# A list scheduler that plans each engine's order: another model of the DMA queue in its play-through

## The chip, the cores and the metric

The kernel runs on one core of a Trainium2 chip. The metric is the device time of one execution in microseconds (us); a kernel's time is the median of several executions. TensorE is called PE in the profile, VectorE DVE, ScalarE ACT, GpSimd POOL and SyncE SP.

## The reference

For batch 8, 8 heads, 576 positions and head size 64, a causal attention with a window of 64 positions is followed by a gated channel mix over rows of 512 values (all heads side by side):

```python
scores = np.where(mask, scale * (q @ k.T), -1e9)     # mask: 0 <= row - column < 64
attn = exp(scores - max) / (sum + 1e-9)
x = (attn @ v)                                       # heads joined: (8, 576, 512)
x_prev = x shifted by one position within each batch
xk = mu_k * x + (1 - mu_k) * x_prev
xr = mu_r * x + (1 - mu_r) * x_prev
k = np.maximum(xk @ w_k, 0)                          # (8, 576, 1024)
out = sigmoid(xr @ w_r) * ((k * k) @ w_v)
```

q, k and v are float32; the three weights come as 64-bit floats, of which the kernel reads the bits.

## The kernel before

**Tiles.** The 4608 rows (8 x 576) are cut into nine units u of 512 rows, and the 512 columns into four chunks c of 128 (two heads). A pair (u, c) is a *group*, numbered g = 4u + c, 36 in all. For a group, `scores` multiplies q with k in 32 small matmuls (into two banks), `soften` takes row minima (`least`, on DVE; the trace calls them CUSTOM_DVE_ANT_0, the order ISA) and exponentials (`exp`, ACT), `shares` turns the row sums into reciprocals (`rs`), `scale` applies them (POOL or DVE), `flip` transposes the weights on PE, `keep` copies the result out of its bank (`pt`), and `values` multiplies with v; `keep_x` copies that into `xT`.

**Units.** Per unit, `mix` blends xT with itself shifted by one row: `d` on ACT, then DVE, then a split into a high and a low part `xs` (each product is made of three matmuls: high by high, high by low, low by high). `r_units` multiplies with w_r, `k_units` with w_k, then relu, square, split (`ks`), and `v_units` multiplies `ks` with w_v; DVE gates the result and SP stores it. These products, 2160 matmuls of 128x512 in all, are the bulk of PE's work. In the trace they are `bank<-xs,ws` (w_r and w_k) and `bank<-ks,ws` (w_v).

**Weights.** There are 20 chunks of 128 x 512 values, 512 KB each as 64-bit words: four of w_r, eight of w_k, eight of w_v. `decode` turns each into a high and a low float (`ws`): `sign` on ACT, then on DVE `clamp` and three bitwise operations (`shift`, `top`, `low`), through a bank, then `first_part` on ACT and `second_part` on POOL or DVE. Only one chunk at a time may be between `shift` and `low` (room "bits": 1).

**What sets the order.** The code does not issue instructions as it goes. Every step is a `Piece` (L82) with an engine (or a choice of two), a key (its due place), a cost in ns, the pieces it needs, and the buffers it takes and frees. `play()` (L96) then plays through the whole program against these costs: on each engine, whenever it is free, the piece with the lowest key begins whose needs are done and landed and whose buffers are free. Behind a piece's end stands its `lag`, the time until others can use what it made. The order in which pieces begin is the order in which the instructions are written (L706), and it is fixed: each engine takes its instructions strictly in this order on the chip, whatever comes late. All instructions are issued through one helper, so the profile gives L69 for nearly all of them.

**Loads.** All loads and stores are issued by SP. `transfer` (L266) makes the piece of a load. The loads at the start have no key and go first, in the order of the calls at L652 to L665: the k and q of groups 0 to 3, the v of groups 0 to 3, the four chunks of w_r between them, then eight chunks of w_k and eight of w_v. For these, `transfer` adds the bytes up at 300 bytes a ns and gives each the sum as its landing time. The loads of groups 4 and up carry a key (one or two places ahead of their group's `burst`), go as soon as their buffer is free, and are taken to land 2000 ns after they are issued, whatever is in the queue ahead of them. An issue costs SP 60 ns in the plan. Groups 2 and 3 have buffers of their own for k and q (`qks`, from the pool of `xs`), so group 4 uses the buffer of group 0 and group 5 that of group 1.

**Bursts.** `burst` is PE's piece of attention: scores of a group, transposes of another, values of a third. The first four have keys -30 to -27, group 4 has -8 (`begin`, L668).

Of the kernel before, what the change touches and what calls it, by code (L numbers as in the profile page):

```python
# [14 lines left out]
ALU = mybir.AluOpType  # L15
PSUM = bass.MemoryType.PSUM

P = 128
# [6 lines left out]
UB = 8  # L25
NU = B * NB // UB
TU = UB * W
# [16 lines left out]
LINK = 80  # L44

HI_MIN = struct.unpack("<f", struct.pack("<I", 0x38000000))[0]
HI_MAX = struct.unpack("<f", struct.pack("<I", 0x47EFFE00))[0]
# [3 lines left out]
def attn_rwkv_kernel(ctx, tc, qT, kT, v2, mu_k, mu_r, w_k, w_v, w_r, out):  # L51
# [9 lines left out]
    class Engine:  # L61


        def __init__(self, engine):
            self.engine = engine
# [5 lines left out]
    pe, dve, sca, pool, dma = (Engine(e) for e in (nc.tensor, nc.vector, nc.scalar, nc.gpsimd, nc.sync))  # L71
    room = {"tmp": TB, "bank": 8, "m": 4, "bits": 1, "s": 2, "t": 2, "x": 1, "pr": 4, "sums": 4, "pt": 4, "xT": XB,
            "xs": SB, "r": R_BUFS, "qk": 2, "v": 3}
    pieces = []
# [7 lines left out]
    class Piece:  # L82


        def __init__(self, engine, key, cost, fn, needs=(), takes=(), uses=(), lag=LINK, spare=0, port=False):
            self.costs = engine if isinstance(engine, dict) else {engine: cost}
            self.home = next(iter(self.costs))
            self.engine, self.key, self.fn = None, key, fn
            self.needs = [p for p in needs if p is not None]
            self.takes, self.uses, self.lag, self.spare, self.port = list(takes), list(uses), lag, spare, port  # L90
            for hold in (*self.takes, *self.uses):
                hold.users.append(self)
            self.done = None
            pieces.append(self)

    def play():  # L96

        left, free, now, begun, port = {}, {}, 0, [], 0
        for n, p in enumerate(pieces):
            for e in p.costs:  # L100
                left.setdefault(e, []).append((p.key, n, p))
                free[e] = 0
        for e in left:
            left[e].sort(key=lambda x: (x[2].home != e, *x[:2]))
        users = {id(h): len(h.users) for p in pieces for h in p.takes}
        ends = []
        times = [0]
        while any(left.values()):
            assert times, [(e, [(p.key, p.fn.__name__) for _, _, p in ps[:4]]) for e, ps in left.items()]
            now = heapq.heappop(times)  # L110
            while ends and ends[0][0] <= now:
                _, _, p = heapq.heappop(ends)
                for hold in (*p.takes, *p.uses):
                    users[id(hold)] -= 1
                    if not users[id(hold)]:
                        room[hold.tag] += 1
            for e, ps in left.items():
                if free[e] > now:
                    continue
                for _, n, p in ps:  # L120
                    if not all(q.done is not None and q.done + (q.lag if q.engine != e else 30) <= now for q in p.needs):
                        continue
                    tags = [h.tag for h in p.takes]
                    if any(room[tag] < tags.count(tag) + (p.spare if tag == "m" else 0) for tag in set(tags)):
                        continue
                    locks = e == "POOL" or (e == "DVE" and p.port)
                    if locks and port > now:
                        continue
                    if p.home != e and max(free[p.home], now) + p.costs[p.home] < now + p.costs[e]:
                        continue  # L130
                    for o in p.costs:
                        left[o].remove((p.key, n, p))
                    for tag in tags:
                        room[tag] -= 1
                    p.engine = e
                    free[e] = p.done = now + p.costs[e]
                    if locks:
                        port = p.done
                    begun.append(p)
                    for at in (p.done, p.done + 30, p.done + p.lag):  # L140
                        heapq.heappush(times, at)
                    heapq.heappush(ends, (p.done + p.lag, n, p))
                    break
        return begun
# [5 lines left out]
        return 150 + 0.52 * n  # L150

    def act_ns(n):
        return 95 + 0.86 * n

    def pool_ns(n):
        return 195 + 2.1 * n
# [1 line left out]
    engines = {"DVE": dve, "POOL": pool}  # L158
# [63 lines left out]
    def decode(n, loaded):  # L222
        ws, _, i, c = chunks[n]
        key = DECODE[n]
        word, bits = Hold("tmp"), [Hold("bank"), Hold("bits")]

        def sign(e):
            words[n] = tmp.tile([P, WC], F32, name="wt", tag="tmp", bufs=TB)
            sca.activation(words[n], raw[n][:, :, 1].bitcast(F32), AF.Abs)

        def clamp(e):
            dve.tensor_scalar(words[n], words[n], HI_MIN, HI_MAX, op0=ALU.max, op1=ALU.min)

        def shift(e):
            words[n, 0] = bank(WC).bitcast(U32)
            dve.tensor_scalar(words[n, 0], words[n].bitcast(U32), 3, 0x3FFFFFF8,
                              op0=ALU.logical_shift_left, op1=ALU.bitwise_and)

        def top(e):
            dve.scalar_tensor_tensor(words[n, 0], raw[n][:, :, 1], 0xC0000000, words[n, 0],  # L240
                                     op0=ALU.bitwise_and, op1=ALU.bitwise_or)

        def low(e):
            dve.scalar_tensor_tensor(words[n].bitcast(U32), raw[n][:, :, 0], 29, words[n, 0],
                                     op0=ALU.logical_shift_right, op1=ALU.bitwise_or)

        def first_part(e):
            ws[i, c] = const.tile([P, 2, WC], F32R, name="ws", tag="w", bufs=len(chunks))
            sca.copy(ws[i, c][:, 0], words[n])

        def second_part(e):
            engines[e].tensor_sub(ws[i, c][:, 1], words[n], ws[i, c][:, 0].bitcast(F32))

        p = Piece("ACT", key, 600, sign, [loaded], takes=[word])
        p = Piece("DVE", key, 430, clamp, [p], port=True)
        p = Piece("DVE", key, 700, shift, [p], takes=bits)
        p = Piece("DVE", key, 700, top, [p])
        p = Piece("DVE", key, 700, low, [p], uses=bits)
        p0 = Piece("ACT", key, 560, first_part, [p])
        decoded[id(ws), i, c] = p0, Piece({"POOL": 1270, "DVE": 700}, key, 0, second_part, [p0], uses=[word], port=True)  # L260


    loaded, arrived, held = {}, {}, {}
    bus = [0]

    def transfer(fn, size, takes=(), needs=(), key=None):  # L266

        p = Piece("SP", len(pieces) - 9999 if key is None else key, 60, fn, needs, takes, lag=2000)
        if key is None:
            bus[0] = max(bus[0], 1300) + size / 300  # L270
            p.lag = bus[0] + 900
        return p


    groups = [(u, c) for u in range(NU) for c in range(NC)]
# [29 lines left out]
    def load_qk(g, key=None):  # L305
        u, c = groups[g]
        held[g] = [Hold("xs" if g in (2, 3) else "qk")]

        def load(e):
            if g in (2, 3):  # L310
                both = act.tile([P, 2, TU], F32, name="qks", tag="xs", bufs=SB)
                loaded[g] = [both[:, 0], both[:, 1]]
            else:
                loaded[g] = [ld.tile([P, TU], F32, name="q"), ld.tile([P, TU + 2 * W], F32, name="k")]
            q, k = loaded[g]
            for b, k0, k1, o in key_loads[u]:
                dma.dma_start(k[:, o * W:(o + k1 - k0) * W], kT[b * NP + c, :, k0 * W:k1 * W])
            o = 0
            for b, i0, i1 in stretches(u):
                n = i1 + 1 - i0  # L320
                dma.dma_start(q[:, o * W:(o + n) * W], qT[b * NP + c, :, i0 * W:(i1 + 1) * W])
                o += n

        arrived[g] = transfer(load, 4 * P * 2 * TU, held[g], key=key)

    def load_v(g, key=None):
        u, c = groups[g]
        held["v", g] = [Hold("xs" if g == 3 else "v")]

        def load(e):  # L330
            if g == 3:
                loaded["v", g] = act.tile([P, UB, P], F32, name="vs", tag="xs", bufs=SB)
            else:
                loaded["v", g] = ld.tile([P, UB, P], F32, name="v", bufs=3)
            for b, a, c0, c1, o in value_loads[u]:
                dma.dma_start(loaded["v", g][:, o:o + c1 - c0], v2[b * NP + c, :, a, c0:c1])

        arrived["v", g] = transfer(load, 4 * P * P * UB, held["v", g], key=key)

    banks, weights, sums, flipped = {}, {}, {}, {}  # L340
    xTs, got = {}, {}
# [316 lines left out]
    load_v(1)  # L658
    load_w(1)
    load_qk(3)  # L660
    arrived["mu"] = Piece("DVE", -25, 300, rest, [transfer(vectors, 4096)])
    load_v(2)
    load_w(1)
    load_v(3)
# [74 lines left out]
```

## Time and profile before

| | us |
|---|---|
| median of 3 executions | 698.28 (697.80 to 699.03) |
| the profiled execution | 697.61 |
| its span, first to last instruction | 695.8 |
| TensorE busy | 633.5 |
| DVE busy | 413.8 |
| ACT busy | 415.6 |
| POOL busy | 112.8 |

The page gives one execution, divided into 40 equal slices; a digit is the busy share of an engine in tenths. A timeline row has the start, the duration, the engine, the line, the operation with its output and inputs, a count of merged instructions and, in brackets, the idle time before and what ended it. Busy time of DVE counts overlapping instructions once, so the step from one start to the next can be shorter than an instruction's duration. A row of the waits reads: who waited for whom, total, times, longest.

### The profile page before, as it was taken

To read this page: it belongs to the slowest core of one execution; us is meant where nothing else is said; L and a number is where in the kernel's file an instruction comes from. 1 tells how busy PE (TensorE), PEld (TensorE's weight loads), DVE (VectorE), ACT (ScalarE), POOL (GpSimd) and SP (SyncE) were. 2 spreads that over 40 slices of the span, in tenths; PEclk is the share of its full clock that TensorE was granted. 3 is DMA by queue.
4 is the path that set the end of the run, shared out by engine and by line. 5 is a ranking of instruction groups with operands and counts; after the bars stand their busy time and mean duration, and the time that the engine had idled before them with its cause. 6 is when DMAs were issued, how large, how long until landed. Compare 5 with 4: busy or idle time off the path is not lost.

```text
span 695.8 us, 12937 instructions
## 1 busy us (share of the span) xinstructions
PE 633.5 (91%) x4752; PEld 510.0 (73%) x4752; DVE 413.8 (59%) x1194; ACT 415.6 (60%) x1130; POOL 112.8 (16%) x183
## 2 busy tenths in 40 slices
PE   1058687899999999999999999999999999999997
PEld 0036565787788888888888888888888888888886
DVE  1047999968758556754675467646764676353311
ACT  2049866947887368646754775477647764671540
POOL 2027784520001000200020002000200020000000
PEclk9998999999999999999999999999999999999999
DMA  8952200244122222222122123222322230001001
GB/s 316 401 183 84 56 1 0 72 151 134 59 60 90 90 60 59 90 90 61 59 90 90 60 59 105 76 65 65 114 80 71 67 112 29 1 16 45 1 0 61
DMA packets 47583, 57.87 MB, mean 83 GB/s; under 512 B 7584, under 2 KB 39328, under 8 KB 47520
## 3 DMA queue, kind: packets, MB, share of 16 engines
q1 hardware_dynamic: 47520, 57.04, 25.4%
q8 instruction: 38, 0.62, 0.4%
q14 instruction: 25, 0.20, 0.1%
HBM read 47.58 MB, written 9.44 MB: 82 GB/s over the span
## 4 chain that ended last, share of the span: by engine, by line
PE 79%; DVE 8%; DMA 5%; ACT 3%; issue 2%; POOL 1%; SPq 0%; DVEq 0%
PE bank L69 79%; DVE bank L69 3%; DVE wt L69 2%; DMA w<-w_v 2%; ACT pr L69 1%; DVE pr L69 1%; DMA q<-qT 1%; DMA w<-w_k 1%; DMA qks<-qT 1%; DMA v<-v 1%; DVE d L69 1%; POOL pr L69 1%; DVE r L69 1%; SPq L69 0%; ACT d L69 0%
## 5 line engine op out<-in xcount | busy, mean ns | idle before, releaser
L69 PE MATMUL bank<-xs,ws 128*128 128x512 f32 x1296 | 316.5, 400 | 9.3 <-ACT xs L69 3.5
L69 PEld LDWEIGHTS bank<-xs,ws 128*128 128x128 f32 x1296 | 244.1, 190 | 68.6 <-ACT xs L69 4.7
L69 PE MATMUL bank<-ks,ws 128*128 128x512 f32 x864 | 209.1, 396 | 1.7 <-ACT xT L69 1.7
L69 PEld LDWEIGHTS bank<-ks,ws 128*128 128x128 f32 x864 | 161.6, 188 | 38.8 <-ACT xT L69 2.1
L69 ACT ACTIVATE pr<-pr,nmax 128x128 f32<-128x128 f32 x288 | 111.9, 393 | 42.5 <-DVE nmax L69 42.4
L69 DVE TENSOR_TENSOR ks<-kf,ks 128x512 fp32r<-128x512 f32 x66 | 45.6, 692 | 82.3 <-ACT ks L69 81.0
L69 PE MATMUL bank<-k,q 64*64 64x128 f32 x1088 | 41.5, 289 | 40.0 <-DMA q<-qT 39.4
L69 ACT ACTIVATE kf<-bank 128x512 f32<-128x512 f32 x72 | 43.0, 599 | 48.6 <-PE bank L69 45.9
L69 PEld LDWEIGHTS bank<-k,q 64*64 64x64 f32 x1088 | 32.4, 140 | 52.3 <-DMA q<-qT 35.8
L69 ACT COPY xT<-bank 128x512 f32<-128x512 f32 x35 | 20.6, 588 | 77.0 <-PE bank L69 76.9
L69 DVE SCALAR_TENSOR_TENSOR r<-bank,r 128x512 f32<-128x512 f32 x36 | 24.9, 692 | 60.7 <-PE bank L69 60.6
L69 DVE CUSTOM_DVE_ANT_0 pr<-bank,maskNone 128x128 f32<-128x128 f32 x224 | 53.7, 286 | 10.5 <-PE bank L69 10.5
L69 ACT ACTIVATE th<-bank 128x512 f32<-128x512 f32 x36 | 21.5, 598 | 63.7 <-PE bank L69 59.6
L69 POOL TENSOR_SCALAR pr<-pr,rs 128x128 f32<-128x128 f32 x76 | 31.8, 437 | 162.8 <-ACT d L69 90.9
L69 ACT ACTIVATION_READ_ACCUMULATOR pr<-pr,nmax 128x1 f32 x288 | 54.9, 191 | 0.0
L69 POOL TENSOR_TENSOR kf<-kf 128x512 f32<-128x512 f32 x12 | 12.5, 1041 | 253.9 <-ACT kf L69 253.9
L69 PE MATMUL bank<-ident,pr 128*128 128x128 f32 x288 | 44.1, 290 | 6.1 <-POOL pr L69 3.3
L69 ACT CAST xs<-d 128x512 fp32r<-128x512 f32 x72 | 43.8, 618 | 3.7 <-DVE d L69 1.6
L69 ACT CAST ks<-kf 128x512 fp32r<-128x512 f32 x72 | 44.2, 617 | 1.7
L69 DVE CUSTOM_DVE_ANT_0 pr<-bank,mask 128x128 f32<-128x128 f32 x64 | 17.9, 286 | 44.3 <-PE bank L69 44.3
L69 PEld LDWEIGHTS bank<-pt,v 128*64 128x64 f32 x1120 | 37.2, 142 | 8.2 <-issue 5.5
L69 PE MATMUL bank<-pt,v 128*64 128x64 f32 x1120 | 42.3, 230 | 1.0 <-ACT kf L69 0.5
(54 smaller groups left out, 585.3 us busy)
## 6 DMA issues: line engine op xcount, KB each, us to landing
v<-v SPq DMA_DIRECT2D x31, 192.0 KB, 2.8
w<-w_k SPq DMA_DIRECT2D x8, 512.0 KB, 8.0
w<-w_v SPq DMA_DIRECT2D x8, 512.0 KB, 10.4
v<-v SPq DMA_DIRECT2D x32, 128.0 KB, 2.4
v<-v SPq DMA_DIRECT2D x15, 256.0 KB, 3.9
v<-v SPq DMA_DIRECT2D x36, 64.0 KB, 2.4
w<-w_r SPq DMA_DIRECT2D x4, 512.0 KB, 5.6
outT<-r SPq DMA_DIRECT2D x8, 256.0 KB, 2.0
```

Source lines behind the costliest of these rows:

```text
L69: return lambda *args, **kw: tc.keep_in_program_order(op(*args, **kw))
```

## The change

In the play-through a piece may now have a `size`. When a piece with a size begins, `play()` keeps one running time for the bus: the later of the bus's time and the end of issue, plus the bytes at 380 a ns; the load lands 2000 ns after that. This goes for every transfer made by `load_w`, `load_qk`, `load_v` and `vectors`, with a key or without; a store keeps its fixed lag of 2500 ns. An issue costs 470 ns for each DMA that the piece issues (`dmas`) instead of 60 ns. Two edits go with it: the plan's cost of an ACT operation is 95 + 0.94 n ns instead of 95 + 0.86 n, and `clamp` takes the minimum first and then the maximum, with its engine given as a choice of one.

```diff
-        def __init__(self, engine, key, cost, fn, needs=(), takes=(), uses=(), lag=LINK, spare=0, port=False):
+        def __init__(self, engine, key, cost, fn, needs=(), takes=(), uses=(), lag=LINK, spare=0, port=False, size=0):
...
-        left, free, now, begun, port = {}, {}, 0, [], 0
+        left, free, now, begun, port, bus = {}, {}, 0, [], 0, 0
...
+                    if p.size:
+                        bus = max(bus, p.done) + p.size / 380
+                        p.lag = bus - p.done + 2000
...
     def act_ns(n):
-        return 95 + 0.86 * n
+        return 95 + 0.94 * n
...
-            dve.tensor_scalar(words[n], words[n], HI_MIN, HI_MAX, op0=ALU.max, op1=ALU.min)
+            engines[e].tensor_scalar(words[n], words[n], HI_MAX, HI_MIN, op0=ALU.min, op1=ALU.max)
...
-        p = Piece("DVE", key, 430, clamp, [p], port=True)
+        p = Piece({"DVE": 430}, key, 0, clamp, [p], port=True)
...
-    bus = [0]
-
-    def transfer(fn, size, takes=(), needs=(), key=None):
-
-        p = Piece("SP", len(pieces) - 9999 if key is None else key, 60, fn, needs, takes, lag=2000)
-        if key is None:
-            bus[0] = max(bus[0], 1300) + size / 300
-            p.lag = bus[0] + 900
-        return p
+
+    def transfer(fn, size, takes=(), needs=(), key=None, dmas=1):
+
+        return Piece("SP", len(pieces) - 9999 if key is None else key, 470 * dmas, fn, needs, takes, size=size)
...
-        arrived[g] = transfer(load, 4 * P * 2 * TU, held[g], key=key)
+        arrived[g] = transfer(load, 4 * P * 2 * TU, held[g], key=key, dmas=2 * len(key_loads[u]))
...
-        arrived["v", g] = transfer(load, 4 * P * P * UB, held["v", g], key=key)
+        arrived["v", g] = transfer(load, 4 * P * P * UB, held["v", g], key=key, dmas=len(value_loads[u]))
...
-    arrived["mu"] = Piece("DVE", -25, 300, rest, [transfer(vectors, 4096)])
+    arrived["mu"] = Piece("DVE", -25, 300, rest, [transfer(vectors, 4096, dmas=2)])
```

More of the change, by code (lines that the diff above doesn't have):

```diff
@@ L89, in __init__ @@
             self.needs = [p for p in needs if p is not None]
-            self.takes, self.uses, self.lag, self.spare, self.port = list(takes), list(uses), lag, spare, port
+            self.takes, self.uses, self.lag, self.spare, self.port, self.size = list(takes), list(uses), lag, spare, port, size
             for hold in (*self.takes, *self.uses):
```

## The prediction

> **What bounds the kernel now.** I read the page first, then the timelines of the load queue and of TensorE, then the chain and the waits, then stretches of time.
>
> The page: engine totals and the span in 40 slices of 17.4 us.
>
> ```profile
> span 695.8 us, 12937 instructions
> PE 633.5 (91%) x4752; PEld 510.0 (73%) x4752; DVE 413.8 (59%) x1194; ACT 415.6 (60%) x1130; POOL 112.8 (16%) x183
> PE   1058687899999999999999999999999999999997
> DVE  1047999968758556754675467646764676353311
> DMA  8952200244122222222122123222322230001001
> ```
>
> PE is full from the ninth slice to the end; of its 62.3 us of idle time (695.8 - 633.5) nearly all lies before. In the second slice every engine but DMA stands at or near 0; after it DVE is full for four slices while PE is not. So there are two stages to explain: a stop, and a start-up carried by DVE.
>
> TensorE's timeline (start, duration, engine, operation, count, idle before and its releaser), then the end of the chain of waits:
>
> ```profile
> 4.22 1.98 PE L69 MATMUL bank<-k,q 64*64 64x128 f32 x32 [4.22 <-DMA q<-qT]
> 41.38 2.44 PE L69 MATMUL bank<-k,q 64*64 64x128 f32 x32 [35.18 <-DMA q<-qT]
> ...
> 127.25 7.24 PE L69 MATMUL bank<-ks,ws 128*128 128x512 f32 x30 [1.66 <-ACT xT L69]
> 134.43 1.10 PE L69 MATMUL bank<-k,q 64*64 64x128 f32 x32
> ```
> ```profile
> 34.14 7.20 DMA q<-qT
> ...
> 181.18 510.90 PE bank L69 x3661
> 692.10 0.69 DVE r L69
> ```
>
> After one group's scores PE stands 35.18 us for the load of a q. The load queue shows which:
>
> ```profile
> 2.59 0.43 SPq L69 DMA_DIRECT2D q<-qT  x1
> ...
> 9.57 0.33 SPq L69 DMA_DIRECT2D qks<-qT  x1
> ...
> 13.32 0.34 SPq L69 DMA_DIRECT2D w<-w_r  x1
> ...
> 15.96 3.94 SPq L69 DMA_DIRECT2D w<-w_k  x8
> 20.79 9.94 SPq L69 DMA_DIRECT2D w<-w_v  x8
> 31.74 1.49 SPq L69 DMA_DIRECT2D k<-kT  x2
> 34.14 1.58 SPq L69 DMA_DIRECT2D q<-qT  x2
> ```
>
> It is group 4's, issued at 34.14 behind all weights and landing at 41.34, while groups 1 to 3 (last issue 9.57) have long landed but stand behind group 4 in PE's order. The others stop with it, each in its own order:
>
> ```profile
> POOL pr L69 <- DVE rs L69: 41.6, 2, 39.9
> DVE pr L69 <- PE bank L69: 37.9, 3, 35.8
> ACT pr L69 <- DVE nmax L69: 34.2, 3, 33.9
> ```
>
> **The change part by part.** What moves: PE's order at its start, before. k_118/q_117 are group 0's, k_124/q_123 group 1's, qks_132 holds group 2's; k_204/q_203 are group 4's.
>
> ```order
> L69 MATMUL bank_185<-k_118,q_117 64x128
> ...
> L69 MATMUL bank_227<-k_204,q_203 64x128
> ...
> L69 MATMUL bank_284<-ident_73,pr_209 128x128 x4
> L69 MATMUL bank_297<-ident_73,pr_214 128x128 x4
> L69 MATMUL bank_310<-k_124,q_123 64x128
> ```
>
> The same place now; qks_168 is group 3's, k_397/q_396 are group 4's.
>
> ```order
> L69 MATMUL bank_135<-k_118,q_117 64x128
> ...
> L69 MATMUL bank_183<-k_124,q_123 64x128
> ...
> L69 MATMUL bank_248<-qks_132 64x128
> ...
> L69 MATMUL bank_354<-qks_168 64x128
> ...
> L69 MATMUL bank_691<-k_397,q_396 64x128
> ```
>
> Group 4 went from second to fifth, behind three groups, their transposes and values, and 45 matmuls of the first products. On DVE, row minima of group 4 (bank_227) stood ahead of the first weight's decode (wt_259):
>
> ```order
> L69 ISA pr_214,nmax_210<-bank_186,maskNone_78 128x128
> L69 ISA nmax_210 128x1
> L69 ISA pr_254,nmax_255<-bank_227,mask1_103 128x128
> L69 ISA nmax_255 128x1
> L69 ISA pr_261,nmax_255<-bank_228,mask1_103 128x128
> L69 ISA nmax_255 128x1
> L69 TENSOR_SCALAR rs_212<-sums_211 128x8
> L69 RECIPROCAL rs_212<-rs_212 128x8
> L69 TENSOR_SCALAR wt_259<-wt_259 128x512
> ```
>
> Now the decode of the first weight (wt_163) comes first, then group 1's minima (bank_183):
>
> ```order
> L69 ISA pr_165,nmax_159<-bank_136,maskNone_78 128x128
> L69 ISA nmax_159 128x1
> L69 TENSOR_SCALAR wt_163<-wt_163 128x512
> L69 TENSOR_SCALAR bank_201<-wt_163 128x512
> L69 SCALAR_TENSOR_TENSOR bank_201<-w_121,bank_201 128x512
> L69 ISA pr_213,nmax_214<-bank_183,mask0_92 128x128
> ```
>
> Nothing here asks for a load behind w_v. So the stop goes, and what is late next is DVE's own list. I use one mark that both orders share: the first ks matmul (third product, first unit) is PE's 253rd row in both, with the same bursts and products ahead of it. Before it starts at 127.25. Stretches up to there (columns: length, busy PE, PEld, DVE, ACT, POOL, granted clock, DMA share, GB/s):
>
> ```profile
> 8.10:44.00 35.90, 2.44 (x32) 1.86 (x32) 0.08 (x3) 2.33 (x11) 0.00 (x0) 1.00 0.94 367
> 44.00:91.10 47.10, 36.57 (x350) 26.88 (x350) 43.19 (x144) 41.79 (x127) 32.96 (x54) 0.93 0.24 66
> 91.10:127.10 36.00, 28.88 (x162) 21.17 (x162) 35.19 (x53) 25.15 (x46) 24.80 (x24) 0.91 0.07 19
> ```
>
> From group 0's minima (done 8.1) to the mark, DVE works 0.08 + 43.19 + 35.19 = 78.5 us, ACT 69.3, PE 67.9, POOL 57.8. Begun at 8.1, DVE's list is the longest, so DVE sets the mark. After 44.0 it idles 83.1 - 78.4 = 4.7 us.
>
> DVE's groups from 43.9 to 127.1 (count, busy, mean ns), and single instructions nothing disturbed:
>
> ```profile
> L69 DVE SCALAR_TENSOR_TENSOR bank<-w,bank 128x512 uint32<-128x512 uint32 x19 | 13.2, 695 | 0.5
> L69 DVE TENSOR_SCALAR wt<-wt 128x512 f32<-128x512 f32 x20 | 11.3, 591 | 0.0
> L69 DVE SCALAR_TENSOR_TENSOR r<-th,r 128x512 f32<-128x512 f32 x4 | 4.7, 1183 | 0.1
> L69 DVE SCALAR_TENSOR_TENSOR d<-xT,mur,d 128x512 f32<-128x512 f32 x4 | 4.3, 1079 | 0.2 <-ACT d L69 0.2
> L69 DVE TENSOR_TENSOR ws<-wt,ws 128x512 fp32r<-128x512 f32 x1 | 1.7, 1664 | 0.0
> ```
> ```profile
> 6.79 0.28 DVE L69 CUSTOM_DVE_ANT_0 pr<-bank,maskNone 128x128 f32<-128x128 f32 x1
> ...
> 7.00 0.29 DVE L69 CUSTOM_DVE_ANT_0 pr<-bank,maskNone 128x128 f32<-128x128 f32 x1
> ...
> 54.97 0.75 DVE L69 SCALAR_TENSOR_TENSOR d<-xT,mur,d 128x512 f32<-128x512 f32 x1
> ...
> 113.02 0.42 DVE L69 TENSOR_SCALAR r<-r 128x512 f32<-128x512 f32 x1
> ...
> 134.72 1.29 DVE L69 TENSOR_TENSOR ks<-kf,ks 128x512 fp32r<-128x512 f32 x2
> ```
>
> The lists differ. Before, 56 bitwise operations of the decode lie ahead of the mark; in the new order 51 do, counting to DVE's row 229, which the order puts beside the mark: -5 x 0.69 = -3.4. Group 6's eight minima now lie ahead: +8 x 0.21 (step 6.79 to 7.00) = +1.7. Seven more subtractions, scalings and copies fall to DVE: +7 x 0.65 (1.29 for two) = +4.5. Sum +2.8.
>
> Some rows above run longer than undisturbed: clamps 20 x (0.59 - 0.42) = 3.4, r<-th 4 x (1.18 - 0.69) = 2.0, blends 4 x (1.08 - 0.75) = 1.3, ws 1.0; with r and th (eight, about 0.28 each, 2.2) some 9.9 us over 41 operations that read and write no bank: 0.24 each. The operations that touch a bank stay at 0.69. Six of the seven new ones are of the exposed kind: +6 x 0.24 = +1.4. The Trainium skill, "SBUF — State Buffer", section "Who interferes with whom", says that VectorE and GpSimd share one port pair as a lock, which a VectorE instruction with two SBUF inputs or in a 2-port mode holds or waits for whole. The split in these rows agrees; by that rule alone an added operation could lose a full GpSimd instruction, an estimate of 6 us instead of 1.4, if each met one.
>
> The mark then: 8.1 + 78.5 + 2.8 + 1.4 + 4.7 = **95.5** against 127.25: 31.7 us earlier. The stall of 35.18 is not won whole, since DVE begins with longer lists and a little fresh contention.
>
> Do loads hold it up instead? Times to landing by the page:
>
> ```profile
> w<-w_k SPq DMA_DIRECT2D x8, 512.0 KB, 8.0
> w<-w_v SPq DMA_DIRECT2D x8, 512.0 KB, 10.4
> w<-w_r SPq DMA_DIRECT2D x4, 512.0 KB, 5.6
> ```
>
> The fourth w_r lands near 13.3 + 5.6 = 18.9, the first w_k near 24.0, the last w_v near 41, group 4's q at 41.3; SP's order is the same up to group 4's loads. DVE has some 19 us of work ahead of the first w_k, so it comes there at 27 or later; group 4's minima stand at DVE's row 117, after roughly 31 us of steps, 39 at the earliest and 43 with its share of waits. The load hides within 3 us, covered by the 4.7. Cost 0; without that cover up to 3.
>
> After the mark: the remaining work on PE is identical, so 695.8 - 127.25 = 568.5 us stay. DVE carries 9 bitwise operations there (6.2 us) instead of 4 (2.8), +3.4, while PE has 11 products and a burst before needing the last weights. I take 0; uncovered it is 3.4.
>
> The other edits: the ACT cost (0.94 for 0.86 per element), dmas and size are planning numbers and run nothing. The clamp swaps its two bounds; same operation and shape, 0 either way. Later load and store order differs by one store moved behind loads; PE has no such wait there, 0.
>
> Sum: span 95.5 + 568.5 = 664.0. The profiled execution took 697.61, 1.8 outside its span: 665.8. It stands 0.67 below the median of 698.28, so I forecast **666.5**.
>
> **Bounds.** If all disturbance and idle vanished (9.9 + 1.4 + 4.7 = 16.0): 650.5. If disturbance and waits doubled (+11.3, +4.7) and the 3.4 were uncovered: 685.9.
>
> **Rivals.**
>
> *Handing over binds (0.12).* In 44.0 to 91.1 ACT is busy 41.79 and DVE 43.19 of 47.1: both nearly full. Packed into 8 to 44, the 32 exponentials of groups 0 to 3 may come in series with the decode:
>
> ```profile
> L69 ACT ACTIVATE pr<-pr,nmax 128x128 f32<-128x128 f32 x288 | 111.9, 393 | 42.5 <-DVE nmax L69 42.4
> ```
>
> 32 x 0.393 = 12.6: 679. Against it: the same mix ran with 4.7 us idle before.
>
> *The disturbance doubles (0.08).* POOL scales four groups' rows early, when DVE decodes; at 0.48 us for each of 47 exposed operations +11.3: 678.
>
> *Nothing disturbs (0.05).* 650.5 to 655; against it, POOL's work is the same.
>
> *The change does not do what it says (0.03).* Another late load stands where group 4 stood, 698. The order speaks against it.
>
> *The clock, on the other side (0.03).* PE's granted clock is 0.93 and 0.91 in the two pieced stretches and full later:
>
> ```profile
> 182.00:220.00 38.00, 38.00 (x282) 30.91 (x281) 24.76 (x83) 30.16 (x87) 2.65 (x6) 1.00 0.28 83
> ```
>
> If the pieced stage, now from 4 us on, left the 565 dense microseconds at 0.93, they would cost 565 x (1/0.93 - 1) = 42.5 more: 709, slower. It turns at 0.947, where 565 x (1/c - 1) equals 31.7. Against it: the clock recovered before. The Trainium skill, "TensorE: Matmul & The Clock Gate", Part 1, says that the array falls to half rate after about 3.4 us idle and is full again after as long a busy time. The 32 matmuls took 1.98 at the start and 1.10 at 134.43, which agrees, though the granted clock reads 1.00 at both; by that rule the dense stretch stays fast.
>
> **How the numbers follow.** My forecast has 0.69, with 655 to 677 of its own; handing over and disturbance reach to 680. Range 655 to 680: some 2 in 10 lie outside. 0.2% (1.4 us) is about what a measurement of this kernel can tell from no change. Faster: 0.69 + 0.12 + 0.08 + 0.05 = 0.94; same 0.02 (no effect, most of it); slower 0.04 (the clock, and a little of no effect).
>
> **What would show it.** In the changed profile: PE's wait of 35 us before its second burst gone, group 1 starting near 7 to 9; DVE busy in the second slice; the first ks matmul near 95, DVE about 83 us busy from 8.1 to there; from it to the end some 568 us. Wrong would be: a new wait of over 5 us on a load after 10; idle PE of over 4 us after the mark; DVE idle by over 10 us between 8 and the mark (handing over); a granted clock under 0.95 after it.

## The result and the profile after

| | before | after |
|---|---|---|
| median of 4 executions, us | 698.23 (697.80 to 699.03) | 666.73 (665.06 to 669.12) |
| ratio | 1 | 0.955 [0.952, 0.958] |
| the profiled execution and its span | 697.61, 695.8 | 666.93, 665.2 |
| first ks matmul (the mark) | 127.25 | 93.92 |
| from the mark to the end of the span | 568.5 | 571.3 |

Of the 30.6 us that the span lost, 33.3 went ahead of the mark, and 2.7 came back behind it. (One execution of e11 took 1570 us, with its products at about twice their usual duration, and one of the kernel before, beside e5 to e8, took 1603; the ratios leave both out, and without its slow one e11's median of 665.81 is 665.67.)

The page after, engine totals and the span in slices of 16.6 us:

```profile
span 665.2 us, 12913 instructions
...
PE 634.0 (95%) x4752; PEld 509.7 (77%) x4752; DVE 413.8 (62%) x1199; ACT 414.6 (62%) x1124; POOL 109.4 (16%) x184
...
PE   4877889989999999999999999999999999999997
...
DVE  4999997696676467546755585548554766272311
```

The busy times are close to those of before. The second slice, empty before, now reads 8 for PE and 9 for DVE: the stop is gone.

TensorE's timeline after, with the bursts of groups 0, 1, 4 and 5, and the mark:

```profile
4.22 1.98 PE L69 MATMUL bank<-k,q 64*64 64x128 f32 x32 [4.22 <-DMA q<-qT]
8.76 1.99 PE L69 MATMUL bank<-k,q 64*64 64x128 f32 x32 [2.56 <-DMA q<-qT]
...
42.44 1.10 PE L69 MATMUL bank<-k,q 64*64 64x128 f32 x32
...
49.11 2.08 PE L69 MATMUL bank<-k,q 64*64 64x128 f32 x30 [3.38 <-DMA v<-v]
...
93.92 7.86 PE L69 MATMUL bank<-ks,ws 128*128 128x512 f32 x33
```

Group 1 starts at 8.76, after 2.56 us for its q, and group 4's scores run at 42.44 without a wait. Group 5's waited 3.38 us at 49.11. The row puts this down to a load of v, but scores don't read v, and group 5's own k and q, issued at 40.76 to 42.08, took at most 3.6 us to land. What ended just then, at 49.06, is `low` on DVE, the last step of a decode, and the wait of the same matmuls' weight loads names it:

```profile
PEld bank L69 <- DVE wt L69: 3.6, 1, 3.6
```

So TensorE waited there for DVE's decode, by all appearances for the bank that it held. In e2 the row of the same place names DVE's wt itself (1.70 us).

Stretches after, up to the mark and behind it (columns as before):

```profile
8.10:93.90 85.80, 66.80 (x544) 51.04 (x545) 80.18 (x221) 71.49 (x201) 47.25 (x70) 0.86 0.55 202
93.90:127.20 33.30, 33.30 (x320) 27.15 (x319) 25.07 (x81) 19.20 (x61) 7.84 (x18) 1.00 0.28 88
```

DVE is busy 80.18 of 85.80 us and idle 5.6. TensorE's clock was not full all the way: the last 24 matmuls ahead of the mark took 7.41 us in after, at a granted clock of 0.76, and 5.86 in the run e7 described below, at 1.00. So some 1.5 us of the mark are the clock.

```profile
86.67 7.41 PE L69 MATMUL bank<-xs,ws 128*128 128x512 f32 x24 [1.64 <-ACT kf L69]
```
```profile
87.69 5.86 PE L69 MATMUL bank<-xs,ws 128*128 128x512 f32 x24 [1.71 <-ACT kf L69]
```

DVE's groups in the first stretch of after (count, busy, mean ns):

```profile
L69 DVE TENSOR_SCALAR bank<-wt 128x512 uint32<-128x512 uint32 x19 | 13.0, 683 | 0.0
L69 DVE SCALAR_TENSOR_TENSOR bank<-w,bank 128x512 uint32<-128x512 uint32 x18 | 12.4, 690 | 0.3
L69 DVE SCALAR_TENSOR_TENSOR wt<-w,bank 128x512 uint32<-128x512 uint32 x18 | 12.3, 684 | 0.3
L69 DVE TENSOR_SCALAR wt<-wt 128x512 f32<-128x512 f32 x20 | 11.6, 602 | 0.0
...
L69 DVE SCALAR_TENSOR_TENSOR r<-th,r 128x512 f32<-128x512 f32 x4 | 3.8, 939 | 0.1
```

The bitwise operations number 19 + 18 + 18 = 55; clamps take 602 ns where before's took 591.

The chain after, from where it leaves DVE to the end (start, duration, engine, output):

```profile
75.04 0.94 DVE wt L69 x2
...
76.00 0.63 ACT ws L69
...
76.69 1.82 POOL ws L69
...
86.67 41.99 PE bank L69 x348
...
141.23 1.65 DVE r L69
142.88 0.61 DVE xs L69
143.53 517.85 PE bank L69 x3740
```

DVE carries it, with short gaps, from 42.4 to 76.0. From there to 86.67 it goes through ACT and POOL, and behind that PE runs through the mark without an external wait. At 128.66 it leaves PE once more, for ACT and DVE, and comes back at 143.53. The waits there are one part of the 2.7 us; the runs below show the other.

### The profile page after: what moved, and what is told of

Its sections match the earlier page's. It is cut to its first block, busy times and chain, and to the rows that moved or that the text cites. A ratio compares the mean times of both kernels' runs of the same rounds, so it can differ in the third digit from the quotient of the medians.

```text
span 665.2 us, 12913 instructions
## 1 busy us (share of the span) xinstructions
PE 634.0 (95%) x4752; PEld 509.7 (77%) x4752; DVE 413.8 (62%) x1199; ACT 414.6 (62%) x1124; POOL 109.4 (16%) x184
## 4 chain that ended last, share of the span: by engine, by line
PE 84%; DVE 6%; DMA 6%; issue 2%; ACT 1%; POOL 1%; SPq 0%; POOLq 0%; DVEq 0%
PE bank L69 84%; DVE bank L69 2%; DMA w<-w_v 2%; DVE wt L69 2%; DMA k<-kT 1%; DMA w<-w_k 1%; DMA qks<-qT 1%; DMA v<-v 1%; DVE r L69 1%; DVE pr L69 1%; ACT kf L69 0%; SPq L69 0%; ACT d L69 0%; DVE d L69 0%; DVE xs L69 0%
## 5 line engine op out<-in xcount | busy, mean ns | idle before, releaser
L69 DVE TENSOR_TENSOR ks<-kf,ks 128x512 fp32r<-128x512 f32 x70 | 48.1, 691 | 82.8 <-ACT ks L69 82.6
L69 PEld LDWEIGHTS bank<-ident,pr 128*128 128x128 f32 x288 | 32.9, 146 | 10.0 <-POOL pr L69 5.5
L69 POOL TENSOR_SCALAR pr<-pr,rs 128x128 f32<-128x128 f32 x76 | 30.0, 417 | 62.1 <-ACT d L69 50.4
(55 smaller groups left out, 568.5 us busy)
```

The source lines that it names most:

```text
L69: return lambda *args, **kw: tc.keep_in_program_order(op(*args, **kw))
```

## The experiments

My theory: the 35 us were the queue ahead of group 4's load; the bus model takes that load out of the way, and DVE's work then sets the mark. The rivals: another of the change's edits did it, or something other than DVE sets the mark. Each ratio below is to the kernel before, run beside it.

### Is it the stop, and whose?

**e1**, before with the new ACT cost alone:

```diff
-        return 95 + 0.86 * n
+        return 95 + 0.94 * n
```

> The kernel before with one edit of the change, the plan's ACT cost of 0.94 per element; group 4's scores stay second in TensorE's order. If the place of group 4's load in the orders carries the gain, the stop of about 35 us stays: 696 to 700. If a more accurate plan of the engines carries it: 685 or less.

Measured 698.19, ratio 1.0002 [0.9991, 1.0012]. TensorE's timeline has the stop:

```profile
42.39 2.43 PE L69 MATMUL bank<-k,q 64*64 64x128 f32 x32 [36.15 <-DMA q<-qT]
```

**e3**, before with both new costs but without the bus:

```diff
-        return 95 + 0.86 * n
+        return 95 + 0.94 * n
...
-        p = Piece("SP", len(pieces) - 9999 if key is None else key, 60, fn, needs, takes, lag=2000)
+        p = Piece("SP", len(pieces) - 9999 if key is None else key, 470 * dmas, fn, needs, takes, lag=2000)
```

> The kernel before with the issue cost of 470 ns for each DMA and the ACT cost of 0.94, landing times as before. Group 4's scores come fourth, behind those of groups 0 to 2; about 12 us of DVE work stand ahead of group 4's minima. Place of group 4: the stop shortens by that work, 698 - 12 = 686 (683 to 690). If the costs carry the gain: 672 or less.

Measured 685.86, ratio 0.9822, within the place of group 4. The stop is shorter, because the order now has groups 1 and 2 ahead of group 4; it ends 1.5 us later than before. TensorE's timeline, then stretches before the stop and behind it:

```profile
42.91 2.40 PE L69 MATMUL bank<-k,q 64*64 64x128 f32 x32 [23.67 <-DMA q<-qT]
```
```profile
8.10:42.90 34.80, 7.63 (x112) 6.08 (x113) 11.59 (x52) 12.43 (x50) 9.66 (x20) 0.71 1.02 392
45.30:116.50 71.20, 54.11 (x399) 40.45 (x397) 68.57 (x148) 54.17 (x129) 44.86 (x49) 0.90 0.12 36
```

DVE got 11.59 us of its 80 done ahead of the stop (before: 0.08), and the mark came at 116.56 instead of 127.25.

**e4**, after, with the loads that have a key taken out of the bus:

```diff
-        return Piece("SP", len(pieces) - 9999 if key is None else key, 470 * dmas, fn, needs, takes, size=size)
+        return Piece("SP", len(pieces) - 9999 if key is None else key, 470 * dmas, fn, needs, takes, lag=2000, size=size if key is None else 0)
```

> The changed kernel, but loads with a key land 2000 ns after issue again, off the bus. Group 4's scores come after the values of group 1; DVE reaches its minima after the first blend, which ran at about 25.8 us in the changed kernel, and then has to wait to about 43.4. Place of group 4: some 16 us slower than the change, 682 (678 to 686), with TensorE idle from about 24 to 41.4. If the other landing times and costs carry the gain: 666 to 670.

Measured 686.21, ratio 0.9828: just above the upper edge. TensorE's timeline:

```profile
42.33 2.38 PE L69 MATMUL bank<-k,q 64*64 64x128 f32 x32 [19.68 <-DMA q<-qT]
```

So it is the loads with a key, the ones that the old model let land 2 us after their issue, that must go through the bus; with the loads at the start alone in it the stop stays. The mark came at 113.22.

**e9**, before's orders on every engine that computes; on SP alone group 4's k and q go ahead of the sixteen chunks of w_k and w_v:

```diff
-    for p in play():
+    row = play()
+    late = [p for p in row if p.home == "SP" and not p.takes and p.fn.__name__ == "load"][4:]
+    row = [p for p in row if p not in late]
+    pos = row.index(arrived[4]) + 1
+    row[pos:pos] = late
+    for p in row:
         p.fn(p.engine)
```

> The kernel before with every compute engine's order untouched; only on SP do the k and q of group 4 stand ahead of the sixteen chunks of w_k and w_v instead of behind them. Theory (the 35.18 us are the queue ahead of the load: the same load with 8 MB less ahead of it ends the stop early): they are issued near 16 to 19 us, land near 21 to 25, PE's second burst then waits 15 to 18 us instead of 35, everything up to the mark (first ks matmul) comes 16 to 20 us earlier, mark 107 to 112, time 676 to 683. Rival (the position of group 4 in the orders costs the time whatever its load does, since the other engines' lists behind it are what is slow): under 5 us gained, 693 to 698. Rival (group 5's load, still behind w_v, stops PE next): a new wait for a q of over 5 us near 43, 684 to 690.

Measured 676.72 (675.64 to 679.01), ratio 0.9699 [0.9679, 0.9718]. TensorE's timeline, then the stretches:

```profile
20.56 2.43 PE L69 MATMUL bank<-k,q 64*64 64x128 f32 x32 [14.34 <-DMA q<-qT]
...
105.83 7.24 PE L69 MATMUL bank<-ks,ws 128*128 128x512 f32 x30 [1.66 <-ACT xT L69]
```
```profile
8.10:23.00 14.90, 2.43 (x32) 1.86 (x32) 0.07 (x2) 2.35 (x11) 0.00 (x0) 1.00 1.05 381
23.00:105.80 82.80, 64.04 (x512) 46.84 (x512) 78.52 (x196) 66.93 (x171) 58.01 (x78) 0.94 0.37 137
```

The stop lost 20.84 us (35.18 to 14.34), the mark 21.42, the span 21.4. DVE's 78.5 us behind the stop and its idle 4.3 are close to before's 78.4 and 4.7. Every engine that computes keeps before's order, and only SP's differs, so the queue is shown to be the cause of these 20.8 us; the 14.34 left end with the landing of the same load. The wait and the mark came some 1 us below the bounds I gave, the time within its range. The change goes 11.9 us further than e9, since it also fills the time of the load with other groups' work. The stop, the mark and the median over the runs:

| | stop | mark | median |
|---|---|---|---|
| before | 35.18 | 127.25 | 698.23 |
| e1 | 36.15 | 128.10 | 698.19 |
| e3 | 23.67 | 116.56 | 685.86 |
| e4 | 19.68 | 113.22 | 686.21 |
| e9 | 14.34 | 105.83 | 676.72 |
| after | none | 93.92 | 666.73 |

### Which edit gives, and which takes?

**e2**, after with both old costs, so the bus alone; **e7** with only the ACT cost old, **e8** with only the issue cost old. e2 has both lines, e7 the first and e8 the second:

```diff
-        return 95 + 0.94 * n
+        return 95 + 0.86 * n
...
-        return Piece("SP", len(pieces) - 9999 if key is None else key, 470 * dmas, fn, needs, takes, size=size)
+        return Piece("SP", len(pieces) - 9999 if key is None else key, 60, fn, needs, takes, size=size)
```

> The changed kernel with the issue cost back at 60 ns and the ACT cost back at 0.86; only the landing by the common bus time is left. Group 4's scores stand behind four groups' attention and 30 matmuls. Place of group 4: 664 to 671. If issue cost and ACT cost carry the gain: 680 or more.

> The changed kernel with the ACT cost back at 0.86 (issue cost kept at 470). The orders of all engines but SP are those of the kernel with the bus alone. If the ACT cost is what makes the change some 4 us slower than the bus alone: 661 to 664. If the issue cost is: 665 to 668.

> The changed kernel with the issue cost back at 60 (ACT cost kept at 0.94). The orders of all engines but SP are those of the changed kernel; group 5's k and q are issued ahead of group 4's v. If the ACT cost is what costs 4 us: 665 to 668. If the issue cost is, or TensorE's wait of 3.4 us on group 5's load: 661 to 664.

| | median | ratio | mark | span behind the mark | of it PE busy |
|---|---|---|---|---|---|
| e2, bus alone | 662.28 | 0.9483 [0.9467, 0.9499] | 93.88 | 568.4 | 563.4 |
| e7, bus and issue cost | 663.20 | 0.9501 [0.9479, 0.9523] | 93.39 | 568.4 | 563.5 |
| e8, bus and ACT cost | 666.50 | 0.9552 [0.952, 0.9584] | 94.04 | 571.1 | 565.0 |
| after, all | 666.73 | 0.955 [0.952, 0.958] | 93.92 | 571.3 | 565.2 |

e2 came out below the 664 to 671 I expected; e7 and e8 lie where an ACT cost to blame puts them. The bus gives all of the gain. The ACT cost takes 3.5 us (after against e7) to 4.2 (e8 against e2) of the median back, and in the profiled executions 2.6 to 2.9 of that lies behind the mark. With the bus in, the issue cost moves only SP's order: the orders of the other engines are the same with it and without. Without the bus it moved more, since e3 differs from e1 by it alone, and there it put two groups ahead of group 4.

What the ACT cost does to the order there is seen in after on three engines, TensorE, POOL and DVE, at the end of the second unit's blends:

```profile
143.53 6.33 PE L69 MATMUL bank<-xs,ws 128*128 128x512 f32 x26 [1.90 <-DVE xs L69]
```
```profile
140.85 1.48 POOL L69 TENSOR_TENSOR xs<-d,xs 128x512 fp32r<-128x512 f32 x1 [10.38 <-ACT xs L69]
```
```profile
139.84 0.69 DVE L69 TENSOR_TENSOR xs<-d,xs 128x512 fp32r<-128x512 f32 x1
...
141.23 1.65 DVE L69 SCALAR_TENSOR_TENSOR r<-th,r 128x512 f32<-128x512 f32 x1
142.80 1.28 DVE L69 TENSOR_TENSOR xs<-d,xs 128x512 fp32r<-128x512 f32 x2
```

The order now has the output's gating (r, th) between the splits xs that PE waits for, and gives one of the splits to POOL. POOL's split runs from 140.85 to 142.33; DVE's r<-th, begun at 141.23, takes 1.65 instead of 0.69, and PE waits 1.90 us. In e2 DVE does five splits in one go at 135.02, and PE waits 0.48 and 0.74 there. The Trainium skill, "SBUF — State Buffer", section "Who interferes with whom", says that a VectorE instruction with two SBUF inputs contends with a GpSimd instruction that reads SBUF, that the ports they share are an exclusive lock, and that the order of issue decides who blocks. The row agrees: it lost 0.96 us, within the 1.10 that POOL's still had to run.

These waits are not the whole price. PE's waits of 1.90 and 0.35 in after stand against 0.48 and 0.74 in e2, which makes 1.0 of the 2.9 us. Most of the rest is PE itself, which is busy 1.8 us longer with the same matmuls; the last section shows where. That e8 pays the same, and e2 and e7 don't, ties it to the order; why the order makes the matmuls longer stays open.

### What sets the mark once the stop is gone?

**e5**, after without the clamp's instruction (the limits on the weights are left out of the computation):

```diff
-            engines[e].tensor_scalar(words[n], words[n], HI_MAX, HI_MIN, op0=ALU.min, op1=ALU.max)
+            return
```

> The changed kernel with the clamp of each weight chunk left out (20 operations on DVE; the decode does without its bounds), all orders otherwise the same. If DVE's list sets the mark: the mark at 93.9 comes earlier by 20 x 0.34 (its undisturbed step) to 20 x 0.60 (its mean with disturbance), 6.8 to 12, so 655 to 660. If handing over through ACT or TensorE sets it: less than 3 earlier, 664 or more.

Measured 661.13 (659.12 to 662.88), ratio 0.947; the mark at 87.30, 6.6 earlier, both just short of what I expected. Only 5.1 of the 6.6 are work left out: the last 24 matmuls start at 81.60 instead of 86.67 and take 5.86 us instead of 7.41, at a granted clock of 1.00. That puts the effect between the theory and the rival. The stretch up to the mark:

```profile
8.10:87.00 78.90, 63.03 (x543) 48.13 (x544) 68.86 (x199) 68.80 (x197) 44.32 (x67) 0.94 0.60 220
```

DVE lost 11.3 us of work, but 4.4 of it turned into idle time (10.0 against 5.6): ACT, at 68.80, is now as long. DVE was the bound, with some 5 us to the next.

**e6**, after, with the bitwise operations in place in SBUF instead of through a bank:

```diff
-            words[n, 0] = bank(WC).bitcast(U32)
+            words[n, 0] = words[n].bitcast(U32)
```

> The changed kernel with the three bitwise operations of the decode in place in SBUF instead of through a bank; orders otherwise the same. If DVE's disturbance comes to operations without a bank while POOL works: the shift gets shorter (0.42 for 0.69), but some 57 more operations are exposed at 0.24 each: 57 x 0.24 - 20 x 0.27 = 8 slower, 670 to 676. If the disturbance has nothing to do with banks: 5 to 7 faster, 660 to 662.

Measured 677.12 (674.70 to 678.80), ratio 0.9698, just above the range; the mark at 105.77, 11.9 later, where I expected 8. Of that 10.7 lie ahead of the last 24 matmuls, which took 8.59 us here. Two of DVE's groups:

```profile
L69 DVE SCALAR_TENSOR_TENSOR wt<-w,wt 128x512 uint32<-128x512 uint32 x34 | 31.2, 917 | 0.6
L69 DVE TENSOR_SCALAR wt<-wt 128x512 uint32<-128x512 uint32 x18 | 14.1, 784 | 0.0
```

The operations of two inputs took 917 ns for 684 to 690 through a bank, and the scalings of pr on POOL rose from a mean of 401 to 578. The disturbance is of operations that leave the banks alone, as the prediction read it, and it goes both ways: POOL's operations take longer too.

**e10**, the bus alone, with the bursts of groups 4 to 7 later:

```diff
-        return -30 + k if k < 4 else 10 * k - 60 if k >= JOINED + 2 else (-8, 0, 6, 12)[k - 4]
+        return -30 + k if k < 4 else 10 * k - 60 if k >= JOINED + 2 else (6, 12, 17, 22)[k - 4]
```

> The bus model alone (662.3 us) with the keys of the bursts of groups 4 to 7 moved later (6, 12, 17, 22 instead of -8, 0, 6, 12), so that fewer row minima, scalings and copies of these groups stand ahead of the first ks matmul on DVE. Theory (DVE's list sets the mark): mark at 88 to 92 instead of 93.9, and if the second unit does not run short of its blends 657 to 661. Rival (what is left out ahead of the mark is owed before the second unit starts): mark earlier, but a new wait of 3 to 10 us on PE between 130 and 165, 662 to 670. Rival (ACT or PE sets the mark): mark unchanged, 661 to 664.

Measured 663.13 (662.73 to 665.24), ratio 0.9506 [0.9489, 0.9523]: no better than e2. The first ks matmul came at 85.06, but ahead of the remaining xs products, so it isn't the same mark. Up to 93.9 PE was busy 66.47 us where e2 has 64.83; the 1.6 gained are given back at the second unit, where PE waits 3.23 us, and the 36 matmuls behind that take 10.49 us, where e2's 36 took 8.62:

```profile
134.20 1.94 PE L69 MATMUL bank<-ident,pr 128*128 128x128 f32 x8 [3.23 <-ACT xs L69]
```

That is the rival: work moved past the mark is owed before the second unit starts.

**e11** and, for its profile, **e12**: the bus alone, with eight clamps on POOL:

```diff
-        p = Piece({"DVE": 430}, key, 0, clamp, [p], port=True)
+        p = Piece({"POOL": 1270} if n >= 4 and n % 2 else {"DVE": 430}, key, 0, clamp, [p], port=True)
```

> The bus model alone (662.3 us) with eight of the twenty clamps given to POOL, which has 47 of 86 us busy ahead of the mark, instead of DVE. Theory (DVE's list sets the mark and can be shortened): DVE loses 8 x 0.60 = 4.8 us, mark 89 to 91, 657 to 661. Rival (work on POOL slows DVE's exposed operations, as in the run with the bit operations in place, and a clamp on POOL takes some 1.3 us): half or all of it is given back, 661 to 666 or above, with DVE's remaining clamps and blends longer than 0.60 and 1.07.

> The same kernel as in the run before (eight clamps on POOL), whose one profiled execution cannot be read for places: for a profile. Its time is 665.8 where the bus model alone took 662.3. Theory (what POOL does slows DVE's exposed operations): the mark stands at 93 or later although eight clamps of 0.60 left DVE; DVE's remaining clamps take over 0.65 and POOL's clamps over 1.2 each. Rival (DVE's list got shorter and the loss lies after the mark): mark at 89 to 92 and waits of 5 us or more on PE after it. Rival (POOL itself is late): PE or DVE waits 3 us or more for a clamp of POOL ahead of the mark. Time again 664.5 to 666.5.

Measured 665.81 and 664.88, ratios 0.953 [0.9516, 0.9544] and 0.952 [0.9504, 0.9536], against 0.9483 of e2: somewhat slower. The stretch up to 93.9 in e12, one group of DVE and one of POOL:

```profile
8.10:93.90 85.80, 61.91 (x541) 47.78 (x545) 78.39 (x213) 68.75 (x198) 48.49 (x73) 0.90 0.56 202
```
```profile
L69 DVE TENSOR_SCALAR wt<-wt 128x512 f32<-128x512 f32 x12 | 8.7, 736 | 0.2 <-ACT wt L69 0.2
```
```profile
L69 POOL TENSOR_SCALAR wt<-wt 128x512 f32<-128x512 f32 x7 | 4.9, 695 | 11.5 <-ACT wt L69 11.3
```

DVE's own clamps rose from 611 (e2) to 736 ns, as the theory has it; POOL's took 695, not over 1.2 us. DVE's busy time fell by 2.3 us (80.69 to 78.39) and its idle time rose by as much. PE did less by 93.9 (61.91 against 64.83), with waits of 4.19, of 3.24 for pr and of 1.89 for ws of POOL. The row of the 4.19, at 44.85, names a load of v, which these matmuls don't read; DVE's ws ended at 44.80, having taken 1.75 us, where e2's two took 0.68 each. That fits the disturbance, since POOL's xs ran from 41.18 to 45.93. No wait is for one of POOL's clamps, as the third rival has it, but POOL's pr and ws came late, so POOL has a part. The first ks matmul came at 98.07, in another order than e2's, so it isn't the same mark. Moving work off DVE's list (e10, e12) did not make the kernel faster, while leaving work out (e5) did. So "DVE sets the mark" holds as a sum; as a chain it does not, since the last part runs through ACT and POOL.

## Why the prediction was right

**The stop.** Right: 35.18 us of waiting for group 4's q are gone, and e9 takes 20.8 of them away by the queue alone. Group 1 started at 8.76, within 7 to 9.

**What is late next.** Right as a sum, too simple as a mechanism. The mark came at 93.92 for 95.5, with DVE busy 80.2 for 82.7 and idle 5.6 for 4.7. DVE's own part of the chain ends at 76.0; then come 10.7 us of handing over between ACT and POOL, and PE's last matmuls. DVE meanwhile worked on pieces for later, so its busy time still fills the stretch; that its sum gave the mark to 1.6 us is in part luck. By 90.9 us DVE was through the 229 rows that the sum prices, 4.6 us early; the sum also has no term for PE's clock, which made the last 24 matmuls some 1.5 us longer.

**The terms of that sum.** Two were wrong and cancelled. The bitwise operations ahead of the mark were 55, not 51, so -0.8 us for -3.4: PE's mark isn't tied to DVE's row 229, and DVE had run past it. The disturbance did not grow by 1.4, it shrank: r<-th took 3.8 us for 4.7, th 1.7 for 2.8, and with all the other rows that makes 2.3 less. The seven more subtractions, scalings and copies cost 3.9 (12 in 8.3 us, against 5 in 4.4) for 4.5. The eight minima cost 2.8 in durations, 0.9 when the overlap that the busy time counts once (1.9 more than before) is taken off, for 1.7. Sum: -0.8 + 0.9 + 3.9 - 2.3 = +1.7 for +4.2, as 80.2 - 78.5 by the stretches.

**Loads.** Right. Group 4's load was hidden, and behind group 2's scores (1.70 us at 12.45) no load stopped PE ahead of the mark. The 3.38 us at group 5's scores, whose row names a load, were a wait for DVE; e8 has it too (3.53), though it issues group 5's k and q ahead of group 4's v.

**After the mark.** Here is the step that was mis-sized: 568.5 was forecast and 571.3 measured. The failed sentence is that the ACT cost is a planning number and runs nothing. By itself it runs nothing, but the order that it plans is run: it put waits of 1.90 and 0.35 ahead of the second unit, where e2 has 0.48 and 0.74, and PE's matmuls took 1.8 us longer. With the old ACT cost (e2, e7) 568.4 stays, the forecast to 0.1. PE's idle time from the mark to its last matmul, 2.3 us, stayed under the 4 named as a sign of being wrong. The 3.4 us of extra bitwise work, taken as 0, did not show: the late decode had 1, not 5, operations more to do.

**The clamp's swapped bounds.** Priced at nothing. Its row reads 602 ns for 591, within what the disturbance explains; no run had it alone, so this is argued, not shown.

**The rivals.** Handing over: DVE idled 5.6, not over 10, so it did not bind in sum, though e5 shows that it is some 5 us behind. The disturbance is real as a mechanism (e6), but it shrank here instead of doubling. The clock read 1.00 behind the mark, not 0.93; ahead of it, over the whole stretch, it read 0.86. The two errors, -1.6 at the mark and +2.8 behind it, leave +1.2 in the span, 665.2 for 664.0. That the median is only 0.2 us off the forecast is partly luck: the profiled execution stands 0.2 above its median, where before's stood 0.6 below.

## What to carry to other kernels

Here the model of a shared queue was worth more than the accuracy of single costs: one load taken to land 2 us after its issue, behind 8 MB that were already queued, put the wrong group second on every in-order engine and cost 31 us. After such a stop goes, the next bound is found by adding each engine's work over the same stretch, but the last steps of the chain are to be read too: here ACT stood within 9 us of DVE, and the chain ended on it. A cost that seems to change nothing but a plan changes the order, and is to be run by itself: here it cost 3.5 to 4.2 us that the bus had won. And a releaser named in a row is to be held against what the instruction reads: more than once here a load of v was named, and DVE was waited for.

## What the runs showed of the hardware

TensorE can be slow after a wait of under 2 us, and need not be. After and e8 have the same orders on the engines that compute, and wait 1.90 and 1.92 us at the same place; e8's timeline reads:

```profile
143.61 7.87 PE L69 MATMUL bank<-xs,ws 128*128 128x512 f32 x26 [1.92 <-DVE xs L69]
```

The same 26 matmuls took 7.87 us, where after's took 6.33, and the granted clock from 144 to 152 was 0.79 there and 1.00 in after. The Trainium skill, "TensorE: Matmul & The Clock Gate", Part 1, says that the window over which idleness is judged is some 3.4 us long and runs free of the kernel. By that rule a wait of 1.9 us is too short to slow the array. Here one of 1.92 us was followed by slow matmuls and one of 1.90 was not; no run here shows the window.

Either way the price was the same. Five profiled executions have this wait (1.87 to 1.92 us). In e5 and e8 the 26 matmuls behind it took 7.87 us, and the steady stretch then steps by 17.08 us from group to group, as in e2. In after, e4 and e6 they took 6.30 to 6.33, and the steady stretch steps by 17.13: 20 groups took 342.7 us in after (from 212.72 to 555.39) and 341.6 in e8 (from 214.16 to 555.76), with the granted clock at 1.00 in both. From the mark to the end all five took 571.1 to 571.3 us, where e2 and e7 took 568.4. What makes the one or the other stays open.
